# Two more tiles turned by DMA, and loads and z1 tiles moved, in a kernel that adds a local attention and a gMLP mixer

## The chip, the cores and the metric

The kernel runs on one core of a Trainium2 chip. The metric is device time in microseconds for one execution, the median of several. A core has five engines, each working through its own list in order: TensorE (PE, with PEld for its weight loads), VectorE (DVE), ScalarE (ACT), GpSimd (POOL) and SyncE (SP, which here only issues DMAs). 16 DMA engines move the data.

## The reference

```python
xn = layernorm(x)                                    # x: 2048 x 512
q, k, v = split(xn @ wqkv)                           # 32 heads of 16
# row s looks at the rows s, s-2, ..., s-14:
o = softmax(mask(q . k[s - 2w]) / 4) @ v[s - 2w]     # w = 0..7
a = o @ wo
z = gelu(xn @ w_in)                                  # 2048 x 1376
z1, z2 = z[:, :688], layernorm(z[:, 688:])
b = (z1 * (w_sp @ z2 + b_sp[:, None])) @ w_out       # w_sp: 2048 x 2048
out = x + a + b
```

All inputs and the output are bfloat16.

## The kernel before

The 2048 rows make 16 tiles of 128. The work is cut into named operations (`op_(name, needs, function)`), and five lists written out by hand (`pe`, `act`, `dve`, `pool`, `sp`, L594 to L641) say in which order each engine runs its operations. An engine that comes to an operation whose inputs aren't there waits, and everything behind it in its list waits too. Names carry a tile or block number:

- `x0` to `x12`: loads of x, by SP. `wz0`, `wz1`, `wy`, `wk`, `wq`, `wv`: loads of weights (z2's by ScalarE's queue, the others by SP).
- `b`, `ag`, `gr`, `n`: normalisation of a tile of x, on VectorE and GpSimd; `n` writes the normalised tile.
- The tile is then turned (rows and columns exchanged) into `xnT`, in one of two ways. For tiles under `NPE`, TensorE transposes it (`T`, L216) and ScalarE copies it out of PSUM (`Tc`, L219). For the others, SP issues a transposing DMA (`t`, L199) behind `n`. `tok(i)` names whichever it is, and `ALLX` all of them.
- `z`: the matmuls of z2's half of a tile (L234), `h` its gelu on ScalarE (L251). `y`: those of z1's half, on the same line L234, `yg` its gelu (L314).
- z2's normalisation: for tiles 0 to 7, statistics `zt` and normalisation `zn` on VectorE, root `zr` on GpSimd; for tiles 8 to 15, `sq` on ScalarE (L278), `zs` and `zb` on VectorE (L282 to L284, L293), `zr` on GpSimd (L288, L289), and `zn` on ScalarE (L305).
- `k`, `q`, `v`: eight blocks each of TensorE work (L325, 32 matmuls a block, and each needs all of `xnT`), copied out by ScalarE as `kc`, `qc`, `vc` (L338). `kh`, `vh`: small DMAs that give each partition the rows before its own.
- The attention's logits: products `m` on VectorE (L363) for four chunks c and two halves of the rows, named `m00`, `m01`, `m10` and so on; the first fold `f00` on VectorE, the others by adding DMAs that GpSimd issues (L371); `p` adds the rest up (L376, L378, L379). Then the softmax (`X`, `e`, `u`, `i`, `C`) and the weighted sum of v (`a0.*`, `a1.*`, L430 to L443).
- `W0` to `W7`: the mixing matrix w_sp, by transposing DMAs on SP (L456), two row tiles each, three buffers; `W2` waits for VectorE's `HW`, later ones for a mixing step. `M0` to `M15`: the mixing on TensorE (L479), `G` its copy with bias on ScalarE (L495), `g` the product with z1 on VectorE (L497), `U` its transposing DMA (L484).
- `gf`, `ao`, `gfl`: the output matmuls (L533, L540, L544); `E`, `F`, `S`: copy, sum with x, store. `LO`: loads of wo and w_out. `R`: x again.

The results of z, y, q, k, v and M share three PSUM buffers in turn (`mm`): a block can start when the block three places before it in TensorE's list has been copied out. The buffer of the normalised tiles has eight places, so `n8` to `n15` also need the turn of the tile eight before. The part of ScalarE's list between the gelus of the last y tiles and the mixing is

```python
yg7 yg8 yg9 zn12 yg10 zn13 yg11 zn14 yg12 zn15 yg13 yg14 yg15 EL
```

(`EL` loads ScalarE's table for the softmax), and VectorE's list at that time is

```python
p01 m20 p10 m21 p11 zs12 m30 p20 zb12 m31 p21 p30 X0 p31
```

GpSimd's list in the stretch of the logits is `zr0 zr4 kh2 f01 zr8 f10 kh3 f11 f20 f21 zr12 f30 f31`.

Of the kernel before, what the change touches and what calls it, by code (L numbers as in the profile page):

```python
# [16 lines left out]
NT = S // P  # L17
# [25 lines left out]
def kernel(  # L43
# [15 lines left out]
    G = nc.gpsimd  # L59
# [3 lines left out]
    x2 = A_x.rearrange("b s d -> (b s) d")  # L63
# [46 lines left out]
    z2 = z2_r[:].rearrange("p (i f) -> p i f", i=NT)  # L110
# [42 lines left out]
    def op_(name, after, f):  # L153
        assert name not in do, name
        do[name], needs[name] = f, list(after)

    def tok(i):
        return f"Tc{i}" if i < NPE else f"t{i}"

    NPE = 8  # L160
    ALLX = [tok(i) for i in range(NT)]
    ALLN = [f"n{i}" for i in range(NT)]

# [18 lines left out]
    def norm(eng, i):  # L182
        eng.tensor_scalar(xn[i % 8], xs[:, i, :], mv[:, i, 0:1], rstd[:, i:i + 1], ALU.subtract, ALU.mult)  # L183
# [5 lines left out]
    for i in range(NT):  # L189
# [6 lines left out]
        else:  # L196
            op_(f"n{i}", [f"gr{i}"] + ([tok(i - 8)] if i >= 8 else []), lambda i=i: norm(V, i))
        if i >= NPE:
            op_(f"t{i}", [f"n{i}"], lambda i=i: SP.dma_start_transpose(xnT[:, :, i * P:(i + 1) * P], xn[i % 8]))  # L199
# [330 lines left out]
    def gated_full(i, start, stop, c=slice(0, D)):  # L530
        th, t0 = i // 8, (i % 8) * P
        for m in range(MF):
            PE.matmul(po[i][:, c], uT[th][:, m, t0:t0 + P], wout[:, m, c], start=(start and m == 0), stop=(stop and m == MF - 1))  # L533

    def attention_out(n, start, stop):
        th, s = n // 2, n % 2
        for r in range(2):
            for g in range(4):
                p = slice(32 * g, 32 * g + RN[r])
                PE.matmul(po[groups[n][g]], rest[th][r][p, s * P:(s + 1) * P], wrest[r][p, :],  # L540
                          start=(start and r == 0), stop=False, tile_position=(32 * g, 0))
        for d in range(DH):
            for g in range(4):
                PE.matmul(po[groups[n][g]], op[32 * g:32 * g + 32, th, d, s * P:(s + 1) * P], wo_r[32 * g:32 * g + 32, d, :],  # L544
                          start=False, stop=(d == DH - 1 and (stop or groups[n][g] == groups[3][3])), tile_position=(32 * g, 0))

    U = [[f"U{j}" for j in range(8 * th, 8 * th + 8)] for th in range(2)]
    EVM = [f"G{j}" for j in range(NT)] + ["Bc", "Tc4"]
    for n in (0, 1):
        op_(f"gf{n}", LO + U[0] + EVM, lambda n=n: [gated_full(i, True, False) for i in groups[n]])  # L550
        op_(f"ao{n}", [f"gf{n}", "a0.11"] + [f"V0{g}" for g in range(4)], lambda n=n: attention_out(n, False, True))
# [37 lines left out]
    for n, (t, c) in enumerate(pieces):  # L589
# [1 line left out]
        op_(f"Sl{n}", [f"Fl{n}"], lambda n=n, c=c: (SP, A, SP)[n].dma_start(out2[il * P:(il + 1) * P, c], o_of(il)[:, c]))  # L591


    pe = """wu T0a T0 B wd z0a T1 z0b T2 z1 T3 z2 T4 z3 T5 z4 T6 z5 T7 z6 z7 y0 y1 z8 z9 z10 z11 z12 z13 z14  # L594
        k0 k1 q0 q1 k2 k3 q2 q3 k4 k5 q4 q5 k6 k7 q6 q7
        v0 v1 v2 v3 v4 v5 v6 v7 z15 y2 y3 y4 y5 y6 y7 y8 y9 y10 y11 y12 y13 y14 y15
        M0 M1 M2 M3 M4 M5 M6 M7 M8 M9 M10 M11 M12 M13 M14 M15
        gf0 gf1 ao0 ao1 gf2 ao2 ao3""".split() + [f"gf3.{i}" for i in tail] + ["gfl0", "gfl1", "gfl2"]
    for n in pe:
# [19 lines left out]
    op_("GL", [], lambda: A.preload_act_table(ACT.Gelu_apprx_tanh))  # L619
    op_("EL", ["yg15"], lambda: A.preload_act_table_set("natural_log_exp_and_others"))  # L620

    act = """wz0 wz1 GL Tc0a Tc0 Bc Tc1 Tc2 h0 Tc3 h1 Tc4 h2 Tc5 h3 Tc6 h4 Tc7 h5 h6 h7 yg0 yg1 h8 h9 sq8 h10 h11 sq9 h12 h13 h14 sq10
        kc0 sq11 kc1 qc0 sq12 qc1 kc2 sq13 kc3 sq14 qc2 qc3 kc4 kc5 qc4 qc5 kc6 kc7 qc6 qc7
        vc0 vc1 zn8 vc2 zn9 vc3 zn10 vc4 zn11 vc5 vc6 vc7 h15 sq15
        yg2 yg3 yg4 yg5 yg6 yg7 yg8 yg9 zn12 yg10 zn13 yg11 zn14 yg12 zn15 yg13 yg14 yg15 EL
        e0 G0 i0 G1 e1 i1 G2 G3 G4 G5 G6 G7 G8 G9 G10 G11 G12 G13 G14 G15""".split()
    act += [f"E{i}" for n in (0, 1) for i in groups[n]]
    dve = """b0 ag0 b1 ag1 n0a n0 b2 ag2 n1 b3 n2 ag3 b4 ag4 n3 b5 ag5 n4 b6 ag6 b7 n5""".split()
    for i in range(6, NT):
# [5 lines left out]
    OUT = [i for n in range(3) for i in groups[n]] + tail  # L635
    dve += [f"F{i}" for i in OUT[:12]] + ["Fe"] + [f"F{i}" for i in OUT[12:]] + ["Fl0", "Fl1", "Fl2"]
    pool = ["b16"] + [f"gr{i}" for i in range(NT)] + "zr0 zr4 kh2 f01 zr8 f10 kh3 f11 f20 f21 zr12 f30 f31 LO5 V00 V01 V02 V03".split()
    sp = """x0 x1 x2 x3 x4 x5 x6 x8 wy x12 wk wq wv t8 t9 t10 t11 t12 t13 t14 t15 W0 kh0a kh0b W1 kh1 vh
        W2 W3 LO0 LO1 W4 U0 W5 LO2 LO3 U1 U2 W6 LO4 U3 U4 W7 U5 U6 U7 U8 U9 U10 R0 U11 U12 U13 V10 V11 R1 U14 V12 U15 V13""".split()
    sp += [f"S{i}" for i in OUT] + ["Sl0", "Sl2"]  # L640
    act.append("Sl1")  # L641
# [52 lines left out]
```

## Time and profile before

| | |
|---|---|
| median of 3 runs | 200.33 us (200.26 to 200.45) |
| profiled execution, its own time | 200.27 us |
| span in its profile | 198.5 us, TensorE clock 1.0 throughout |
| TensorE busy | 194.2 us (98%) |
| VectorE busy | 178.4 us (90%) |
| ScalarE busy | 89.4 us (45%) |
| GpSimd busy | 49.3 us (25%) |
| moved by DMA | 32.87 MB, of which read from HBM 10.13 MB |

Times in the profile are microseconds from the start of the span. A row of a timeline has the start, the time from the first to the last of the instructions it merges, the engine (`SPq` is a DMA issue on SP), the line of the kernel, the operation, what it writes and reads, how many instructions, and in brackets how long the engine had been idle before, and what released it. A row of the DMA issues ends with the median time from issue to landing. A row of the chain has start, length, engine and line. A row of the table by stretches has, after the length, the busy time of PE, PEld, DVE, ACT and POOL with the number of instructions, the granted clock, the mean busy share of the DMA engines and GB/s.

### The profile page before, as it was taken

What the parts mean: (1) busy time and instruction counts of PE and PEld (TensorE: products, weight loads), DVE (VectorE), ACT (ScalarE), POOL (GpSimd) and SP (SyncE); (2) the same over time, 40 slices, a digit from 0 to 9 for tenths busy, and PEclk for the clock granted to TensorE, in tenths of its full rate; (3) what the DMA queues carried; (4) which work ended last, traced back from release to release, by engine and by line L of the source; (5) the groups of instructions that cost most, each with busy time, mean ns of one, the idle gap of its engine ahead of it and who ended that gap; (6) DMA issues with size and microseconds to landing.
All of it is one profiled execution on the core that took longest, in us unless ns stands there. A gap on an engine that the chain in (4) does not pass through costs nothing.

```text
span 198.5 us, 4606 instructions
## 1 busy us (share of the span) xinstructions
PE 194.2 (98%) x1957; PEld 122.0 (61%) x1960; DVE 178.4 (90%) x205; ACT 89.4 (45%) x130; POOL 49.3 (25%) x83
## 2 busy tenths in 40 slices
PE   8999999999999999999999999999999999999993
PEld 2566666666666666666666666666666654444442
DVE  4899896999979999988999999999999999997244
ACT  2587797875559885991462311111222110044000
POOL 5567222005992249363000000010111000000000
PEclk9999999999999999999999999999999999999999
DMA  5999566860979999998299999999999969204233
GB/s 156 355 363 212 102 135 137 96 131 6 182 141 173 204 168 179 169 181 162 48 229 229 165 220 236 193 181 225 262 185 109 242 116 259 45 3 147 68 106 106
DMA packets 69076, 32.87 MB, mean 166 GB/s; under 512 B 57312, under 2 KB 67072, under 8 KB 68928
## 3 DMA queue, kind: packets, MB, share of 16 engines
q1 hardware_dynamic: 65680, 24.15, 58.2%
q0 software_dynamic: 2688, 7.70, 21.2%
q10 hardware_dynamic: 688, 0.74, 1.3%
q8 instruction: 15, 0.25, 0.5%
q14 instruction: 5, 0.04, 0.1%
HBM read 10.13 MB, written 2.10 MB: 62 GB/s over the span
## 4 chain that ended last, share of the span: by engine, by line
PE 94%; DMA 2%; DVE 1%; issue 1%; POOL 0%; SPq 0%; DVEq 0%
PE mm L479 38%; PE mm L325 21%; PE mm L234 18%; PE mm L544 7%; PE mm L533 6%; PE aux L533 2%; DMA z<-in_A_x_dram 2%; PE mm L540 1%; PE aux L216 1%; SPq L166 0%; DVE stats L173 0%; DVE z L590 0%; POOL rstd L180 0%; DVE z L183 0%; POOL rstd L179 0%
## 5 line engine op out<-in xcount | busy, mean ns | idle before, releaser
L479 PE MATMUL mm<-z,wsp 128*128 128x344 bf16 x512 | 74.8, 309 | 0.0
L479 PEld LDWEIGHTS <-wsp 128*128 128x128 bf16 x512 | 50.1, 98 | 24.6
L325 PE MATMUL mm<-xnT,wts 128*32 128x512 bf16 x768 | 41.7, 379 | 0.0
L234 PE MATMUL mm<-wts,xnT 128*128 128x344 bf16 x256 | 38.8, 309 | 0.0
L325 PEld LDWEIGHTS <-wts 128*32 128x32 bf16 x768 | 28.5, 138 | 13.0 <-issue 0.3
L430 DVE TENSOR_TENSOR prod<-vp,a_sb 128x4096 bf16<-128x4096 bf16 x16 | 36.2, 2283 | 0.0
L495 ACT ACTIVATE qk<-mm,b_col 128x688 bf16<-128x688 f32 x16 | 13.2, 830 | 42.8 <-PE mm L479 41.3
L234 PEld LDWEIGHTS <-xnT 128*128 128x128 bf16 x256 | 24.7, 98 | 11.8 <-issue 0.4
L363 DVE TENSOR_TENSOR prod<-qk 128x4096 bf16<-128x4096 bf16 x12 | 26.9, 2287 | 0.3 <-ACT qk L338 0.2
L434 DVE TENSOR_TENSOR prod<-prod,prod 128x8192 bf16<-128x8192 bf16 x6 | 26.5, 4420 | 0.1
L338 ACT CAST qk<-mm 128x1024 bf16<-128x1024 f32 x16 | 16.2, 1012 | 8.2 <-PE mm L325 8.2
L490 POOL DMA_DIRECT2D qk<-qk x8 | 3.9, 496 | 54.2 <-DMA qk<-z 49.6
L544 PE MATMUL mm<-wts,xnT 32*128 32x512 bf16 x192 | 14.5, 374 | 0.0
L314 ACT ACTIVATE z<-mm 128x688 bf16<-128x688 f32 x16 | 11.6, 744 | 3.4 <-PE mm L234 3.0
L533 PEld LDWEIGHTS <-qk 128*128 128x128 bf16 x75 | 7.2, 98 | 9.1 <-issue 0.8
L251 ACT ACTIVATE z<-mm 128x688 bf16<-128x688 f32 x16 | 11.9, 745 | 1.8 <-PE mm L234 1.8
L533 PE MATMUL mm<-wts,qk 128*128 128x512 bf16 x52 | 12.2, 379 | 0.3 <-issue 0.2
L173 DVE BATCH_NORM_STATS2 stats<-z 128x6 f32<-128x512 bf16 x16 | 10.7, 671 | 1.7 <-DMA z<-in_A_x_dram 1.7
L371 POOL DMA_DIRECT2D prod<-prod x10 | 9.4, 1132 | 8.4 <-DVE prod L363 8.4
L544 PEld LDWEIGHTS <-xnT 32*128 32x128 bf16 x256 | 6.5, 93 | 7.3
L578 ACT CAST z<-mm 128x512 bf16<-128x512 f32 x6 | 3.3, 600 | 13.7 <-PE mm L544 13.7
L338 ACT CAST vp<-mm 128x1024 bf16<-128x1024 f32 x8 | 8.1, 1011 | 2.7 <-PE mm L325 2.7
(92 smaller groups left out, 186.9 us busy)
## 6 DMA issues: line engine op xcount, KB each, us to landing
prod<-prod POOLq DMA_DIRECT2D x10, 512.0 KB, 8.5
wts<-in_A_wo_dram SPq DMA_DIRECT2D x4, 512.0 KB, 6.7
wsp<-in_A_x_dram SPq DMA_DIRECT2D x2, 1024.0 KB, 6.1
out_dram<-z SPq DMA_DIRECT2D x15, 128.0 KB, 1.8
wts<-in_A_wqkv_dram SPq DMA_DIRECT2D x3, 512.0 KB, 8.8
z<-in_A_x_dram SPq DMA_DIRECT2D x2, 512.0 KB, 6.4
wsp<-z POOLq DMA_DIRECT2D x2, 512.0 KB, 7.1
wsp<-wts POOLq DMA_DIRECT2D x2, 512.0 KB, 9.4
```

What stands on the lines that cost most here:

```text
L234: PE.matmul(t[:, hh, 0:FHALF], xnT[:, kc, i * P:(i + 1) * P], w_z[part][:, kc, hh * FHALF:(hh + 1) * FHALF], start=(kc == 0), stop=(kc == ...
L251: A.activation(z2[:, i, :].rearrange("p (a b) -> p a b", a=2), t[:, :, 0:FHALF], ACT.Gelu_apprx_tanh, **total)
L314: op_(f"yg{i}", [f"y{i}"], lambda: A.activation(z1u[:, i, 0:FH].rearrange("p (a b) -> p a b", a=2), t[:, :, 0:FHALF], ACT.Gelu_apprx_tanh))
L325: PE.matmul(t[32 * g:32 * g + 32, dd, :], w, r, start=(kc == 0), stop=(kc == C - 1), tile_position=(0, 32 * g))
L338: op_(f"{a}c{p}", [f"{a}{p}"], lambda: A.copy(home(a, p), t[:].rearrange("p d (t s) -> p d t s", t=2)))
L363: V.tensor_tensor(pr, q, k, ALU.mult)
L430: return lambda: V.tensor_tensor(dst, vp[:, :, th, off:off + GS], a_sb[:, th, W - 1 - w].unsqueeze(1).broadcast_to([P, DH, GS]), ALU.mult)
L434: return lambda: V.tensor_tensor(dst, dst, x, ALU.add)
L479: PE.matmul(t[:, hh, 0:FHALF], w[:, k, (j % 2) * P:(j % 2 + 1) * P], z2[:, k, hh * FHALF:(hh + 1) * FHALF], start=(k == 0), stop=(k == NT ...
L495: lambda: A.activation(gs[j % 3].rearrange("p (a b) -> p a b", a=2), t[:, :, 0:FHALF], ACT.Identity, bias=b_col[:, j:j + 1]))
L533: PE.matmul(po[i][:, c], uT[th][:, m, t0:t0 + P], wout[:, m, c], start=(start and m == 0), stop=(stop and m == MF - 1))
L544: PE.matmul(po[groups[n][g]], op[32 * g:32 * g + 32, th, d, s * P:(s + 1) * P], wo_r[32 * g:32 * g + 32, d, :], start=False, stop=(d == DH ...
```

## The change

Three things in one:

- `NPE` goes from 8 to 6: tiles 6 and 7 are turned by transposing DMAs (`t6`, `t7`) on SP, ahead of `t8`, in place of `T6` and `T7` on TensorE and `Tc6` and `Tc7` on ScalarE.
- On TensorE, `y2` and `y3` run among the first z tiles and before `k0`; before, they came behind `z15`. Their gelus `yg2` and `yg3` move with them on ScalarE.
- On SP, `wq` is issued behind `t15`, and `wv` behind `kh1`; before, both came ahead of `t8`. `W0` is issued behind `kh0b`, and `W1` behind `wv`.

VectorE's and GpSimd's lists are the same.

```diff
-    NPE = 8
+    NPE = 6
...
-    EVM = [f"G{j}" for j in range(NT)] + ["Bc", "Tc4"]
+    EVM = [f"G{j}" for j in range(NT)] + ["Bc", "Tc5"]
...
-    pe = """wu T0a T0 B wd z0a T1 z0b T2 z1 T3 z2 T4 z3 T5 z4 T6 z5 T7 z6 z7 y0 y1 z8 z9 z10 z11 z12 z13 z14
+    pe = """wu T0a T0 B wd z0a T1 z0b T2 z1 T3 z2 T4 z3 T5 z4 z5 y0 y1 y2 z6 z7 z8 y3 z9 z10 z11 z12 z13 z14
         k0 k1 q0 q1 k2 k3 q2 q3 k4 k5 q4 q5 k6 k7 q6 q7
-        v0 v1 v2 v3 v4 v5 v6 v7 z15 y2 y3 y4 y5 y6 y7 y8 y9 y10 y11 y12 y13 y14 y15
+        v0 v1 v2 v3 v4 v5 v6 v7 z15 y4 y5 y6 y7 y8 y9 y10 y11 y12 y13 y14 y15
...
-    act = """wz0 wz1 GL Tc0a Tc0 Bc Tc1 Tc2 h0 Tc3 h1 Tc4 h2 Tc5 h3 Tc6 h4 Tc7 h5 h6 h7 yg0 yg1 h8 h9 sq8 h10 h11 sq9 h12 h13 h14 sq10
+    act = """wz0 wz1 GL Tc0a Tc0 Bc Tc1 Tc2 h0 Tc3 h1 Tc4 h2 Tc5 h3 h4 h5 yg0 yg1 yg2 h6 h7 h8 sq8 yg3 h9 h10 h11 sq9 h12 h13 h14 sq10
...
-        yg2 yg3 yg4 yg5 yg6 yg7 yg8 yg9 zn12 yg10 zn13 yg11 zn14 yg12 zn15 yg13 yg14 yg15 EL
+        yg4 yg5 yg6 yg7 yg8 yg9 zn12 yg10 zn13 yg11 zn14 yg12 zn15 yg13 yg14 yg15 EL
...
-    sp = """x0 x1 x2 x3 x4 x5 x6 x8 wy x12 wk wq wv t8 t9 t10 t11 t12 t13 t14 t15 W0 kh0a kh0b W1 kh1 vh
+    sp = """x0 x1 x2 x3 x4 x5 x6 x8 wy x12 wk t6 t7 t8 t9 t10 t11 t12 t13 t14 t15 wq kh0a kh0b W0 kh1 wv W1 vh
```

## The prediction

> **What bounds the kernel now.** I read the page first (the busy times), then the chain of work that ended last, in order of time, then the timelines of VectorE and ScalarE around the places where that chain changes line.
>
> ```profile
> PE 194.2 (98%) x1957; PEld 122.0 (61%) x1960; DVE 178.4 (90%) x205; ACT 89.4 (45%) x130; POOL 49.3 (25%) x83
> ```
>
> ```profile
> 12.72 1.17 PE mm L234 x8
> 13.89 0.22 PE aux L216 x4
> 14.11 1.17 PE mm L234 x8
> 15.28 0.22 PE aux L216 x4
> 15.50 12.83 PE mm L234 x88
> 28.34 41.60 PE mm L325 x768
> 69.94 17.61 PE mm L234 x120
> 87.54 74.67 PE mm L479 x512
> 183.70 3.46 PE mm L544 x64
> ```
>
> Columns: start, length, what. TensorE carries the end from 8 us on with hardly a hole: z4, T6, z5, T7, then eleven more z and y tiles (88 matmuls) from 15.50, the 24 blocks of q, k and v from 28.34, z15 and y2 to y15 from 69.94, the mixing M0 to M15 from 87.54, and the output. Taken alone, that says: fewer matmuls, less time. But VectorE, at 90%, is one serial chain beside it, and each engine works through a fixed list. So the question is where TensorE waits for VectorE as soon as VectorE is later. The slack at two such places is small, and the rows for them follow where they are used.
>
> **What TensorE saves.** T6 and T7 go: the two x4 rows above, 2 × 0.22 = 0.44 us, both on the chain. Their ScalarE copies go too; ScalarE was not the bound there, so they count nothing.
>
> **What moves k and q.** y2 and y3 now run before k0 instead of after z15. A z or y tile costs 1.17 us (the x8 rows), so k0 starts at 28.34 − 0.44 + 2 × 1.17 = 30.24, that is 1.90 us later. All q, k, v blocks and z15 follow 1.90 later; y4 then starts 0.44 earlier than before, because y2 and y3 are already done. TensorE's own sum is −0.44. For this to hold, the transposes by DMA must be there in time:
>
> ```profile
> 12.85 0.40 DVE L183 TENSOR_SCALAR z<-z,mv,rstd 128x512 bf16<-128x512 bf16 x1
> 15.24 11.09 SPq L199 DMA_TRANSPOSE xnT<-z  x8
> xnT<-z SPq DMA_TRANSPOSE x1, 4.2
> wts<-in_B_w_in_dram SPq DMA_DIRECT2D x1, 688.0 KB, 6.5
> 5.65 0.37 SPq L246 DMA_DIRECT2D wts<-in_B_w_in_dram  x1
> ```
>
> n6 ends at 13.25, so t6 issues then. Eight issues took 11.09 us, 1.39 each; the first of them landed 4.2 us after issue, behind the weights' loads, and I take that slow value for t6: 17.5. TensorE reaches z6 after z5, y0, y1, y2, at 13.89 + 4 × 1.17 = 18.57. Cover 1.1 us. t15 issues at 13.3 + 9 × 1.39 = 25.8 and lands by 30.0 even at 4.2, against k0 at 30.24. y0 now starts at 15.06 and needs wy, which lands at 5.65 + 6.5 = 12.15. So the turns are hidden; where the cover of z6 is gone, each late microsecond is paid in full, by TensorE and by everything behind k0.
>
> wq issues behind t15, at about 27.2, and q0 needs it at 30.24 + 2 × 1.73 = 33.7 (a block is 41.60/24 = 1.73 us).
>
> ```profile
> z<-in_A_x_dram SPq DMA_DIRECT2D x1, 128.0 KB, 2.2
> wts<-in_A_wqkv_dram SPq DMA_DIRECT2D x1, 512.0 KB, 7.9
> wts<-in_A_wqkv_dram SPq DMA_DIRECT2D x1, 512.0 KB, 10.0
> 10.00:15.00 5.00, 5.00 (x44) 3.45 (x42) 4.93 (x16) 4.48 (x8) 3.58 (x10) 1.00 1.09 364
> ```
>
> Before, wk and wv landed 7.9 and 10.0 us after issue, in the stretch in which the queues moved 364 GB/s (last column) and were full. In the new place the queue holds only the last turns, so the nearer row is the 128 KB load at the very start, 2.2 us, plus 384 KB at 364 GB/s, 1.1 us: 3.3, landing at 30.5. Bounds: 3.3 to 10.0, the upper end making q0 3.5 us late. I take 3.3, cost 0. wv, issued at about 43.5, has until v0 at 30.24 + 16 × 1.73 = 57.9: hidden at either end.
>
> **What VectorE does with 1.90 us.** Its products start when q0 has been copied:
>
> ```profile
> 33.73 1.01 ACT L338 CAST qk<-mm 128x1024 bf16<-128x1024 f32 x1 [0.71 <-PE mm L325]
> 34.81 4.49 DVE L363 TENSOR_TENSOR prod<-qk 128x4096 bf16<-128x4096 bf16 x2 [0.24 <-ACT qk L338]
> 47.13 0.86 POOL L343 DMA_DIRECT2D qk<-qk  x1 [14.16 <-ACT qk L338]
> 48.55 1.86 POOL L371 DMA_DIRECT2D prod<-prod  x2
> 57.90 1.23 DVE L376 TENSOR_TENSOR a_sb<-prod 128x2048 bf16<-128x2048 bf16 x1 [1.21 <-DMA prod<-prod]
> 64.02 1.23 DVE L378 TENSOR_TENSOR wsp<-wsp 128x2048 bf16<-128x2048 bf16 x1 [0.31 <-DMA wsp<-z]
> 80.72 0.15 DVE L293 TENSOR_TENSOR zbias<-zmean,zrstd 128x4 f32<-128x4 f32 x1
> ```
>
> m00 waited for qc0 (the bracket), so it starts 1.90 later. From there to zb12 at 80.72 VectorE idles only 1.21 us at p01 and 0.31 us at p10. Neither wait absorbs the shift: p01 waits for the fold f01, which GpSimd issues behind kh2, which itself waited 14.16 us for ScalarE's copy of k5, and that is 1.90 later too. So zb12 moves by D = 1.90, plus what f01 loses to DMA.
>
> On SP, W0 now runs behind kh0b and W1 behind wv:
>
> ```profile
> 34.95 5.33 SPq L456 DMA_TRANSPOSE wsp<-in_B_w_sp_dram  x1
> wsp<-in_B_w_sp_dram SPq DMA_TRANSPOSE x1, 7.5
> 38.91 1.01 ACT L338 CAST qk<-mm 128x1024 bf16<-128x1024 f32 x1
> vp<-vp SPq DMA_DIRECT2D x1, 96.0 KB, 11.9
> 45.00:50.00 5.00, 5.00 (x100) 3.45 (x96) 4.93 (x7) 2.86 (x4) 2.87 (x4) 1.00 0.09 6
> ```
>
> W0 takes W1's old place (34.95 + 1.90 = 36.85, issued by about 42). kh1 is queued behind it and waits for kc3 at 39.92 + 1.90 = 41.82 anyway. Then wv at 43.5 and W1 at 44, landing at 44 + 7.5 + 1.4 for wv's 512 KB ahead of it (at 364 GB/s) = 52.9. f01 is issued at 48.55 + 1.90 = 50.45, and before it found the DMA engines idle (6 GB/s from 45 to 50). That two queues hinder each other is shown by vh, 96 KB in 11.9 us beside a fold. From f01's issue to W1's landing are 2.4 us, and f01 loses all of that if it stands still so long, nothing if W1's data is through when f01's begins. As data starts after its issue and stops before its landing, I take a value near the lower end, 0.3 (my estimate). The Trainium skill, "DMA: Bandwidth & Descriptors", section "Queues, rings and completion order", says that each DMA engine takes turns between the queues it has work for, a packet at a time; by that rule f01 would run at half speed while W1 lasts, and would lose 1.2 us if the whole 2.4 overlapped. The row of vh agrees that they hinder each other, not on the share.
>
> D = 1.90 + 0.3 = 2.2 us.
>
> **Where TensorE then waits.** ScalarE's list has zn12 between yg9 and yg10, and zn12 needs zb12.
>
> ```profile
> 80.58 0.74 ACT L314 ACTIVATE z<-mm 128x688 bf16<-128x688 f32 x1 [0.42 <-PE mm L234]
> 81.22 0.95 ACT L305 ACTIVATE z<-z,zbias,zrstd 128x688 bf16<-128x688 bf16 x1
> 82.07 0.73 ACT L314 ACTIVATE z<-mm 128x688 bf16<-128x688 f32 x1
> 86.50 2.02 ACT L314 ACTIVATE z<-mm 128x688 bf16<-128x688 f32 x3
> ```
>
> Before, zb12 was done at 80.87, 0.35 us ahead of zn12 at 81.22, and ScalarE then ran without a hole through zn12, yg10, zn13, yg11, zn14, yg12, zn15 and yg13, which ended at about 86.50 + 0.74 = 87.24: 6.02 us after zn12's start. M0 reuses the PSUM buffer that yg13 empties, and started at 87.54. Now zn12 starts at 80.87 + D + 0.05 for the handover, and M0 at 6.02 + 0.05 after it: 86.99 + D. Where D is under 0.1, TensorE's own 87.10 holds; at 0.55 the gain is gone; at 2.2 M0 starts at 89.2, 1.65 us later than before. TensorE first stops at y13, which needs yg10's buffer, then a little at y14, y15 and M0. With two more y tiles done early y10 comes no later than before, but its copy is queued behind zn12.
>
> **Does it stay to the end?** After M0 TensorE is 1.65 late and VectorE 2.2, so margins shrink by 0.55.
>
> ```profile
> 96.86 9.25 SPq L456 DMA_TRANSPOSE wsp<-in_B_w_sp_dram  x2
> wsp<-in_B_w_sp_dram SPq DMA_TRANSPOSE x1, 6.2
> 177.34 2.29 DVE L443 TENSOR_TENSOR xnT<-prod 128x4096 bf16<-128x4096 bf16 x1
> ```
>
> W2, released by VectorE, landed at 96.86 + 6.2 = 103.1; M4 began at 87.54 + 4 × 4.67 = 106.2: margin 3.1, then 2.6. VectorE's last step ended at 179.63 against its reader at 183.70: margin 4.1, then 3.5. Nothing there adds or gives back. The profiled run took 200.27 in all (span 198.5 and 1.8 around it), 0.06 under the median 200.33; 200.27 + 1.65 = 201.92, as a median 201.98, so 202.0.
>
> **The rivals.**
> *TensorE alone decides* (faster; 0.09): 200.33 − 0.44 = 199.9, if D stays under 0.1. For it: the 98% and the chain. Against it: the 0.24 wait of m00 for qc0, and no idle time of VectorE's own to catch up in. The Trainium skill, "Perfetto Trace Analysis", section "Identifying the Most-Contended Engine", takes the engine with the highest occupancy as the one to optimize first; by that rule removing TensorE work pays, 199.9. The busy times agree on which engine that is; the slack of 0.35 us before zn12 is what that rule leaves out.
> *VectorE gives most of it back* (same; 0.06): with W0 gone from the front, f01 lands early and the 1.21 wait at p01 disappears. D = 0.7, net +0.15: 200.5. Against it: f01 had an empty DMA before and can't be quicker.
> *A late load* (slower still; 0.10): wq after 33.7 or t6 after 18.6. Each microsecond shifts m00 too; wq at 6 us, between its bounds, makes nothing late, 8 us makes it 1.5 late: 203.5.
> *W1 holds f01 up in full* (slower still; 0.06): 2.4 instead of 0.3, D = 4.3: 204.1. For it: vh. Against it: the empty queue in front of wv, which lets W1 start at once.
>
> **How the numbers follow.** The forecast case has 0.69 and lies between 201.4 (D 0.3 less and a hand-off or two shorter) and 202.7; the two slower rivals bring slower to 0.85. About 0.2% or 0.4 us is what a measurement of this kernel can tell from no change. The range 200.9 to 203.3 reaches down to D = 1.1 (0.8 of p01's wait absorbed) and up to D = 3.5, f01 losing two thirds of its 2.4; it leaves out faster and same (0.15 together) and the tails of the slower rivals.
>
> **What would show it.** Right: T6 and T7 missing, z6 without a wait, k0 at about 30.2; m00 at 36.7 released by ScalarE's copy; zb12 at about 83; zn12 idle before it by 2 us or so, released by VectorE; TensorE holes of 1 to 2 us in all from y13 to M0 and M0 at about 89.2; f01's wait at p01 between 1.2 and 1.6. Wrong: zb12 before 81.5, or M0 before 87.5; or TensorE idle between 14 and 34, which would say that a turn or wq was late; or M4 or the output waiting for VectorE.

## The result, and the profile after

The changed kernel takes 201.84 us (median of 6, 201.64 to 202.16); the kernel before, in the same series, 200.30. The ratio is 1.0074, with a 95% interval of 1.0057 to 1.0090: slower by 1.5 us. The profiled execution of the changed kernel took 202.16 us, with a span of 200.4 us; it is the longest of its six, so its trace shows some 0.3 us more than the median.

TensorE's timeline of the changed kernel, first up to the k blocks, then from the first hole to the mixing (start, length, what; in brackets the idle time and what ended it):

```profile
12.42 17.66 PE L234 MATMUL mm<-wts,xnT 128*128 128x344 bf16 x120
30.01 10.36 PE L325 MATMUL mm<-xnT,wts 128*32 128x512 bf16 x185
...
84.45 1.33 PE L234 MATMUL mm<-wts,xnT 128*128 128x344 bf16 x8 [1.00 <-ACT z L314]
85.94 1.33 PE L234 MATMUL mm<-wts,xnT 128*128 128x344 bf16 x8 [0.15 <-ACT z L314]
87.42 1.33 PE L234 MATMUL mm<-wts,xnT 128*128 128x344 bf16 x8 [0.15 <-ACT z L314]
88.90 11.39 PE L479 MATMUL mm<-z,wsp 128*128 128x344 bf16 x77 [0.15 <-ACT z L314]
```

From z4 on, 15 tiles run as one piece: no turn came late. The four brackets are y13, y14, y15 and M0: 1.00 + 3 × 0.15 = 1.45 us of holes, all ended by a copy of ScalarE. TensorE loses somewhat more there than it idles: a tile lasts 1.33 us in these rows, and in an unbroken stretch the next one starts 1.17 us after it, so each hole also loses an overlap of 0.16 us: 1.45 + 4 × 0.16 = 2.1 us.

VectorE of the changed kernel, at m00, p01, p10 and zb12:

```profile
36.52 4.49 DVE L363 TENSOR_TENSOR prod<-qk 128x4096 bf16<-128x4096 bf16 x2 [2.06 <-ACT qk L338]
58.74 1.23 DVE L376 TENSOR_TENSOR a_sb<-prod 128x2048 bf16<-128x2048 bf16 x1 [0.34 <-DMA prod<-prod]
65.92 1.23 DVE L378 TENSOR_TENSOR wsp<-wsp 128x2048 bf16<-128x2048 bf16 x1 [1.37 <-DMA wsp<-z]
82.62 0.15 DVE L293 TENSOR_TENSOR zbias<-zmean,zrstd 128x4 f32<-128x4 f32 x1
```

m00 starts 1.71 us later than before, zb12 1.90. The two waits between them have changed places: p01 waits 0.34 instead of 1.21, p10 1.37 instead of 0.31.

ScalarE of the changed kernel, yg9, zn12, yg10, and the end of the series:

```profile
79.99 0.74 ACT L314 ACTIVATE z<-mm 128x688 bf16<-128x688 f32 x1 [0.42 <-PE mm L234]
82.81 0.96 ACT L305 ACTIVATE z<-z,zbias,zrstd 128x688 bf16<-128x688 bf16 x1 [2.08 <-DVE zbias L293]
83.68 0.72 ACT L314 ACTIVATE z<-mm 128x688 bf16<-128x688 f32 x1
...
88.11 2.01 ACT L314 ACTIVATE z<-mm 128x688 bf16<-128x688 f32 x3
```

zn12 waits 2.08 us for zb12, and yg10 stands behind it although y10 was long done. M0 starts at 88.90. Before, it started at 87.38 in the same view (the chain in the prediction has 87.54, because it counts from the end of the tile before):

```profile
87.38 2.79 PE L479 MATMUL mm<-z,wsp 128*128 128x344 bf16 x18
```

So M0 is 1.52 us later: TensorE lost 2.1 us from y13 on, saved 0.44 with T6 and T7, and its first steps came 0.14 earlier in this execution.

And the end, which the prediction hadn't looked at: VectorE's last step, the span and SP's wait for the stores, first of the kernel before, then of the changed kernel.

```profile
195.56 0.28 DVE L590 TENSOR_TENSOR z<-aux,stmp 128x128 bf16<-128x128 f32 x1
core 0: 198.5 us, clock 1.000
SPq L689 <- DMA out_dram<-z: 0.3, 1, 0.3
```

```profile
197.10 0.28 DVE L590 TENSOR_TENSOR z<-aux,stmp 128x128 bf16<-128x128 f32 x1
core 0: 200.4 us, clock 1.000
SPq L689 <- DMA out_dram<-z: 0.8, 1, 0.8
```

From the end of VectorE's last step to the end of the span were 198.47 − 195.84 = 2.63 us before and 200.39 − 197.38 = 3.01 after (spans to two digits): 0.38 us more behind the last computation. So the profiled 1.92 us between the spans are 1.54 up to VectorE's last step and 0.38 behind it.

### The profile page after: what moved, and what is told of

It reads as the page before. It is cut to its first block, busy times and chain, and to the rows that moved or that the text cites. A ratio compares the mean times of both kernels' runs of the same rounds, so it can differ in the third digit from the quotient of the medians.

```text
span 200.4 us, 4594 instructions
## 1 busy us (share of the span) xinstructions
PE 194.4 (97%) x1949; PEld 121.9 (61%) x1952; DVE 178.5 (89%) x205; ACT 88.7 (44%) x128; POOL 49.3 (25%) x83
## 4 chain that ended last, share of the span: by engine, by line
PE 73%; DMA 11%; issue 5%; DVE 4%; POOL 3%; ACT 2%; SPq 0%; DVEq 0%; ACTq 0%; POOLq 0%
PE mm L479 37%; PE mm L234 10%; PE mm L325 9%; PE mm L544 7%; PE mm L533 6%; DMA wsp<-wts 5%; DMA prod<-prod 4%; DVE prod L363 2%; PE aux L533 2%; DMA z<-in_A_x_dram 2%; ACT z L314 1%; POOL prod L371 1%; PE mm L540 1%; DVE a_sb L376 1%; PE aux L216 1%
## 5 line engine op out<-in xcount | busy, mean ns | idle before, releaser
L180 POOL TENSOR_TENSOR rstd<-rstd,mhalf 128x1 f32<-128x1 f32 x16 | 9.0, 561 | 1.3
## 6 DMA issues: line engine op xcount, KB each, us to landing
wsp<-wts POOLq DMA_DIRECT2D x2, 512.0 KB, 10.2
```

## The experiments

Each was measured against the kernel before on the same chip; "over before" is that difference of medians. The ratio comes with its 95% interval.

**e1: y2 and y3 back behind z15**, the rest of the change kept.

```diff
-T5 z4 z5 y0 y1 y2 z6 z7 z8 y3 z9 ... z15 y4
+T5 z4 z5 y0 y1 z6 z7 z8 z9 ... z15 y2 y3 y4
```

> The changed kernel with y2 and y3 (and yg2, yg3) put back behind z15; turns by DMA and the moved loads stay. Theory (the two y tiles ahead of k0 make VectorE late, zn12 waits for zb12, and TensorE stops at y13 to M0): TensorE would reach k0 at 27.7, but t15 lands at 28.5 (25.99 + 2.5 in the trace of after), so k0 starts at about 28.5, VectorE is late by 0.2 and M0 by 0.2 against before: about 200.5, and no wait of zn12 over 0.5 us. Rival (the transposing DMAs or the moved loads cost the time): the cost stays, 201.8 or, with t8 late too, more.

201.16 against 200.42, ratio 1.0034 (1.0014 to 1.0055). k0 starts at 28.5, as the landing of t15 set it, and zn12 doesn't wait:

```profile
28.46 41.67 PE L325 MATMUL mm<-xnT,wts 128*32 128x512 bf16 x768
87.58 12.71 PE L479 MATMUL mm<-z,wsp 128*128 128x344 bf16 x86
```

```profile
80.78 0.74 ACT L314 ACTIVATE z<-mm 128x688 bf16<-128x688 f32 x1 [0.42 <-PE mm L234]
81.42 0.95 ACT L305 ACTIVATE z<-z,zbias,zrstd 128x688 bf16<-128x688 bf16 x1
```

Half of the loss goes with the two y tiles. What is left, 0.7 by the medians, is more than the expected 0.1 to 0.2: in the trace M0 is 0.2 later than before (87.58 against 87.38) and the end 0.4 longer (3.0 us behind VectorE's last step). The rest, some 0.2, is within the interval.

**e3: the kernel before with y2 and y3 alone moved.**

```diff
-T6 z5 T7 z6 z7 y0 y1 z8 z9 ... z15 y2 y3 y4
+T6 z5 T7 y0 y1 y2 z6 z7 z8 y3 z9 ... z15 y4
```

> The kernel before with y2 and y3 (and yg2, yg3) alone moved ahead of k0 (T6 and T7 stay on TensorE, the loads stay). Theory: k0 later by 2 x 1.17 = 2.33, VectorE later by as much, M0 at 86.99 + 2.33 = 89.3 instead of 87.54: slower by 1.8, about 202.1. Rival (turns by DMA or loads are the cause): no change, 200.3.

202.32, ratio 1.0080 (1.0060 to 1.0101): 1.9 us over before by the medians, 1.6 by the ratio, with T6 and T7 still on TensorE and no load moved. The same holes are there (0.52 at y13, then three of 0.15), in an execution in which k0 came as late as 32.2, so only the holes are read from it. So moving two y tiles is enough for the whole loss; the turns and loads give back what TensorE saves or less.

**e4: W0 and W1 in their old places**, the rest of the change kept.

```diff
-t15 wq kh0a kh0b W0 kh1 wv W1 vh
+t15 wq W0 kh0a kh0b W1 kh1 wv vh
```

> The changed kernel with SP's W0 and W1 back in their places before: t15 wq W0 kh0a kh0b W1 kh1 wv vh. It keeps W1 away from the fold f01. Theory: the loads take no part beyond the 0.2 us by which VectorE was late at p10; zb12 at 82.4 to 82.6, time 201.6 to 201.9. Rival (W1 beside the folds costs most of the time): 200.5 to 201.0.

201.93 against 200.42, ratio 1.0081 (1.0049 to 1.0113): 1.5 over before. zb12 starts at 82.56 against 82.62 in the changed kernel. W1 beside the fold is not the cause.

**e2 and e5: zn12 to zn15 later in ScalarE's list.** VectorE stays late, but no gelu stands behind its result.

```diff
-yg9 zn12 yg10 zn13 yg11 zn14 yg12 zn15 yg13 yg14 yg15
+yg9 yg10 yg11 zn12 yg12 zn13 yg13 zn14 yg14 zn15 yg15
```

> The changed kernel with ScalarE's list yg9 yg10 yg11 zn12 yg12 zn13 yg13 zn14 yg14 zn15 yg15 in place of yg9 zn12 yg10 zn13 yg11 zn14 yg12 zn15 yg13 yg14 yg15; VectorE stays as late as it is. Theory: zn12 still waits for zb12 (82.8), but yg10 and yg11 no longer stand behind it, so y13 to M0 run without a hole, M0 at 86.95 instead of 88.90, and the 0.44 us of T6 and T7 come out: about 199.9. M0 reads z2 of tile 12 only 12 x 0.29 us after its start. Rival 1 (M0 waits for all of z2, zn15 ending at 88.4): 201.3. Rival 2 (TensorE waits for VectorE elsewhere, M4 or the output, or the loads cost): 201.8.

227.38, ratio 1.1349 (1.1323 to 1.1376): none of the theories. zn12's place had carried a second order: yg10 to yg15 write where half of the products m10 are kept, and only because zn12 came first were yg10 and yg11 issued behind the fold f10 that reads them. In e2 f10 comes behind them and folds overwritten data, so e2 doesn't compute the reference; and f10 waits for them:

```profile
83.82 1.76 POOL L371 DMA_DIRECT2D wsp<-z  x2 [26.36 <-ACT z L314]
```

e5 has e2's list and holds yg10 to yg15 behind f10 explicitly:

```diff
-op_(f"yg{i}", [f"y{i}"], ...)
+op_(f"yg{i}", [f"y{i}"] + (["f10"] if i >= 10 else []), ...)
```

> The changed kernel with ScalarE's list yg9 yg10 yg11 zn12 yg12 zn13 yg13 zn14 yg14 zn15 yg15, and with yg10 to yg15 held behind the fold f10, which reads products kept in the place that yg10 to yg15 write. VectorE stays as late as it is. Theory: zn12 still waits for zb12 (82.6), but yg10 and yg11 no longer stand behind it; y13 to M0 run without a hole, M0 at 86.95 instead of 88.90, and the 0.44 us of T6 and T7 come out: 0.4 to 0.5 under the kernel before, about 199.9 where before is 200.3. M0 comes to tile 12 of z2 only 12 x 0.29 us after its start. Rival 1 (M0 waits for all of z2, zn15 ending at 88.4): 1.0 over before. Rival 2 (TensorE waits for VectorE elsewhere, or the loads cost): 1.5 over before.

201.38 against 200.25, ratio 1.0064 (1.0050 to 1.0078). The number is near that of rival 1, but M0 waited for nothing: the part up to M0 came out (no hole, M0 at 86.93), the time did not, because there was a next wait. TensorE of e5:

```profile
71.75 15.34 PE L234 MATMUL mm<-wts,xnT 128*128 128x344 bf16 x104
86.93 23.50 PE L479 MATMUL mm<-z,wsp 128*128 128x344 bf16 x160
111.30 51.49 PE L479 MATMUL mm<-z,wsp 128*128 128x344 bf16 x352 [0.87 <-ACT qk L495]
```

The bracket is M5, which reuses the buffer that G2 empties. ScalarE of e5, then of before, then of the changed kernel: i1 (two rows in e5, one of them in the others), and G2 with G3:

```profile
109.66 0.42 ACT L411 ACTIVATE stmp<-stmp 128x256 f32<-128x256 f32 x1 [4.23 <-DVE stmp L408]
110.11 0.42 ACT L412 ACTIVATE stmp<-stmp 128x256 bf16<-128x256 f32 x1
110.43 1.54 ACT L495 ACTIVATE qk<-mm,b_col 128x688 bf16<-128x688 f32 x2
```

```profile
107.99 0.42 ACT L411 ACTIVATE stmp<-stmp 128x256 f32<-128x256 f32 x1 [4.24 <-DVE stmp L408]
108.76 1.54 ACT L495 ACTIVATE qk<-mm,b_col 128x688 bf16<-128x688 f32 x2
```

```profile
110.61 0.42 ACT L411 ACTIVATE stmp<-stmp 128x256 f32<-128x256 f32 x1 [4.24 <-DVE stmp L408]
111.38 1.54 ACT L495 ACTIVATE qk<-mm,b_col 128x688 bf16<-128x688 f32 x2
```

G2 stands behind i1, which waits for VectorE's sum u1. A copy lasts 0.82 us and a mixing step 4.67. Before, G2 was done at 108.76 + 0.82 = 109.6, and M5 began at 87.38 + 5 × 4.67 = 110.7: 1.1 us of slack. In the changed kernel G2 was done at 111.38 + 0.82 = 112.20 and M5 began at 88.90 + 5 × 4.67 = 112.25: 0.05 us of slack. TensorE's own lateness had just kept this wait out of sight.

**e6 and e7: the same ScalarE list without the change, and with the y tiles alone.**

> The kernel before with ScalarE's list alone changed as in e5_zn_later2. Theory: TensorE never waited for zn12 there, so nothing changes: within 0.2 us of before. Rival (the new order is quicker by itself, whatever VectorE does): 0.3 or more under before.

200.13 against 200.25, ratio 0.9993 (0.9982 to 1.0005): the list by itself brings nothing.

> The kernel before with y2 and y3 moved ahead of k0 (as in e3_y_only, 1.6 over before) and ScalarE's list as in e5_zn_later2. Theory: VectorE is as late as in e3_y_only but nothing on TensorE's path waits for it: within 0.2 us of before. Rival (the late k and q cost elsewhere too): 0.5 to 1.6 over before.

201.51, ratio 1.0062 (1.0043 to 1.0080), inside the rival's range: late k and q do cost elsewhere as well. M5 idles 0.81 us there, released by ScalarE as in e5.

**e8: tiles 4 and 5 by DMA too**, on top of e5 (`t4` and `t5` ahead of `t6` on SP, the gelus in the new order).

```diff
-NPE = 6
+NPE = 4
-T3 z2 T4 z3 T5 z4 z5 y0 y1 y2 z6 z7 z8 y3 z9
+T3 z2 z3 y0 y1 y2 y3 z4 z5 z6 z7 z8 z9
```

> e5_zn_later2 with tiles 4 and 5 turned by DMA too (NPE 4) and TensorE's order z3 y0 y1 y2 y3 z4 to z14 k0. Theory: two more turns of 0.22 us leave TensorE, k0 at 29.6, t15 lands by 28.5: 0.8 to 0.9 under the kernel before. Rival (wy lands at 12.15 and t4 behind the loads at 16 to 17, so TensorE waits at y0 or z4): 0 to 0.4 under before.

201.54, ratio 1.0065 (1.0046 to 1.0084), outside both: TensorE's first turns came 0.5 us later in this execution, so that k0 began at 30.2 instead of 29.6 although nothing waited from z2 on; M5 waited 1.44 us for G2, and from VectorE's last step to the end were 2.9 us. This run tells nothing of whether two more turns pay.

**f2: e7 with G2 ahead of e1 and i1.**

```diff
-e0 G0 i0 G1 e1 i1 G2 G3
+e0 G0 i0 G1 G2 e1 i1 G3
```

> e7_y_only_zn (1.25 over before; M5 idle 0.81) with G2 ahead of e1 and i1; turns on TensorE and loads as before. Theory: with both of ScalarE's waits moved, late k and q cost nothing: within 0.2 us of before. Rival (they cost somewhere else as well): 0.4 to 1.2 over before.

200.24 against 200.33, ratio 0.9991 (0.9969 to 1.0013). With both waits moved, the early y2 and y3 cost nothing that shows, though VectorE starts m00 2.5 us later than before (37.36 against 34.81).

**f3: the changed kernel with kh1 issued by GpSimd**, two DMAs fewer on SP.

```diff
-W0 kh1 wv W1 vh           (SP)
+W0 wv W1 vh
-zr0 zr4 kh2 f01           (GpSimd)
+zr0 zr4 kh1 kh2 f01
```

> The changed kernel with kh1 alone moved from SP to GpSimd (ahead of kh2), so that the last store again takes the DMA semaphore that the end waits for last. Theory: time from VectorE's last step to the end 2.6 instead of 3.0 us, the rest as it is: 0.4 under the changed kernel, 1.1 to 1.2 over before. Rival (the 3.0 comes from other transfers still in flight): 3.0 stays, 1.5 over before.

201.58, ratio 1.0049 (1.0026 to 1.0073). Last step and span:

```profile
196.89 0.28 DVE L590 TENSOR_TENSOR z<-aux,stmp 128x128 bf16<-128x128 f32 x1
core 0: 199.8 us, clock 1.000
```

The end is back at 2.6 us, with the holes from y13 to M0 still there (0.70 + 0.16 + 2 × 0.15). By the medians the kernel is 1.25 us over before instead of 1.54: 0.3 less, where 0.4 was expected, and within the intervals of both.

**f1: all three on the changed kernel** (e5's list and hold, G2 as in f2, kh1 as in f3).

> e5_zn_later2 (1.1 over before) with two more edits: G2 ahead of e1 and i1 in ScalarE's list (e0 G0 i0 G1 G2 e1 i1 G3), and kh1 issued by GpSimd (ahead of kh2) instead of SP, which brings SP's number of DMAs back to that of the kernel before. Theory (three waits in a row: zn12, then M5's buffer through G2 behind i1, then the wait at the end for the DMA semaphores in a fixed order): M5 no longer idles (0.87 in e5), the time from VectorE's last step to the end is 2.6 instead of 3.0, and TensorE's 0.44 comes out: 0.3 to 0.5 under before. Rival (TensorE meets the next wait, W2 at M4 or VectorE at the output): 0 to 0.8 over before.

199.86 us (median of 11, 199.52 to 200.36) against 200.33, ratio 0.9964 (0.9933 to 0.9995): the quickest of all, under both kernels.

```profile
12.37 17.66 PE L234 MATMUL mm<-wts,xnT 128*128 128x344 bf16 x120
29.96 41.67 PE L325 MATMUL mm<-xnT,wts 128*32 128x512 bf16 x768
71.56 15.34 PE L234 MATMUL mm<-wts,xnT 128*128 128x344 bf16 x104
86.74 74.83 PE L479 MATMUL mm<-z,wsp 128*128 128x344 bf16 x512
```

One piece from z4 to the end of the mixing. What T6 and T7 cost, 0.44 us, is now about what the kernel gains, 0.47 by the medians. By the interval of the ratio the gain is between 0.1 and 1.3 us, so how near the two figures are tells little.

## Why the prediction was right, step by step

The forecast, 202.0 us, and its mechanism held: k and q come later, VectorE with them, zn12 waits for zb12 in ScalarE's list, and TensorE stops from y13 to M0. That the number was met within 0.2 us is luck in part. Two of its terms were off and nearly cancelled (0.3 for f01, which did not come; 0.38 at the end, which it didn't have), and two waits that it had not priced, at p10 and at M5, happened to leave it standing.

- **Turns and loads in time**: held. t6 landed at 13.14 + 4.1 = 17.2 (17.5 in the prediction), k0 began at 30.0 in the timeline (30.24), wq landed at 27.26 + 4.0 = 31.3 (30.5), ahead of q0 at 33.5. e1 shows the other side: without the two y tiles, t15 would have held up k0.
- **VectorE 1.90 later**: m00 moved by 1.71 in the profile (TensorE's first steps were 0.14 earlier in this execution), zb12 by 1.90.
- **f01's loss to W1, 0.3**: mis-sized and misplaced. W1 landed at 43.76 + 9.6 = 53.4 (52.9 in the prediction), but f01 landed about 1 us sooner after its issue, and p01's wait shrank by 0.87, to 0.34, where the prediction's signs had 1.2 to 1.6. The prediction had excluded that f01 could be quicker; this was wrong. So the condition of the rival *VectorE gives most of it back* came true for the most part, and what let it fall is a wait that neither had priced: p10's wait for f10 grew by 1.06. GpSimd issues f10 behind f01, at 56.99 instead of 55.29, so it came late whatever f01 did. Together VectorE lost 0.19 us, and in e4, with W1 away from the fold, p10 waits 1.10 as well; so W1 isn't what p10 waits for. Why f01 was quicker is open. The moved loads aren't needed for it: in e3 and f2, with the loads in their old places, p01 doesn't wait at all.
- **zn12, y13 and M0**: held. zn12 idle 2.08 us (about 2), holes 1.45 (1 to 2), M0 at 88.90 (89.2). e5 shows the cause: with yg10 and yg11 ahead of zn12, the holes are gone although zb12 comes as late. In the changed kernel the chain of waits names f21's DMA as what released yg10, and that can't be. f21 is two DMAs, issued at 73.23 and 73.77; they took 10.2 us to land in the median and the first one 9.2, so the second took 11.2 and landed at 85.0, when yg10 was already done (83.68 + 0.72). What yg10 stood behind is zn12, which ended at 82.81 + 0.96 = 83.77; yg10 starts 0.09 ahead of that end, as yg11 does with zn13 (0.10).
- **"Nothing there adds or gives back"**: wrong by 0.38 us, the longer end. f3 shows that it comes with the two more DMAs on SP.
- **The margins behind M0**: the prediction let them shrink by 0.55 us. They shrank by about twice that: i1 is 2.62 us later than before (110.61 against 107.99) and M0 1.52, because VectorE lost more behind zb12, first of all at p30, which waits 1.52 for its fold instead of 0.68. M4 and the output had enough and held. The margin of M5 over G2 was overlooked; it went down to 0.05 us, and that it did not run out was luck. In e5 and e7 it does.
- **The other rivals**: nothing was late among the loads, and W1 did not stop f01, so the two for slower still fell. *TensorE alone decides* fell with zb12's 1.90; its time, 199.9, is what f1 takes once the waits are moved.

The Trainium skill, "Perfetto Trace Analysis", section "Identifying the Most-Contended Engine", has one optimize the engine with the highest occupancy first; f1 agrees with this once the waits are gone, since it gains about what was taken off TensorE. In the changed kernel the same saving was there and was lost at an engine, ScalarE, that is busy for 44% of the span. For TensorE the same section goes by MFU (the share of the peak arithmetic rate) and by the busy time of the weight loads instead of that of the matmuls. The weight loads have 61% here and VectorE 90%, so the rule names TensorE less plainly than the prediction took it to.

## What to carry to other kernels

Moving filler work ahead of the producer of a second chain makes that chain late, even if the busiest engine does less; look for each place where the busiest engine reads something that the second chain has touched, and for what stands in order behind it on a third, mostly idle engine. Moving only the position of such an operation in its list can make the delay free, but check which other orders the old position had carried, and look for the next wait of the same kind before expecting the whole gain. Add up what happens behind the last computation as well.

## What the runs showed of the hardware that was not expected

At the end SP waits for the DMA semaphores (the counters that tell that a DMA has landed) one after another, in the same order in every trace here. The single instructions of the trace show it: before and in f1 and f3, the last store counts on the semaphore that is waited for last, and the end follows directly. In the changed kernel, with two more DMAs on SP, the last store counts on the second of those that the list has for SP's and ScalarE's DMAs. That wait ends at 199.12, when the store has landed, and six more follow at 0.06 us each, 0.37 us in all. The four kernels with SP's old number of DMAs and only y tiles or lists changed (e3, e6, e7, f2) have 2.6 us behind VectorE's last step; those with two more (e1, e4, e5 and the changed kernel) 3.0. e8, with four more, fits too: its last store counts two places further on, four waits follow, and it has 2.9. The prediction priced the added DMAs by their place in SP's queue and missed this.
